# Forward and gradients of attention plus a gated layer, one core: which rows of the query, gate and up weights lie in which partition

## The chip, the cores and the metric

The kernel runs on one core of one Trainium2 chip. The metric is device time in microseconds for one execution; where several runs are given, the median. The engines are TensorE (PE, with its weight loads PEld), VectorE (DVE), ScalarE (ACT), GpSimd (POOL) and SyncE (SP), which here does little but issue transfers. The core's 16 DMA engines move all data between HBM and SBUF (128 partitions).

## The reference, cut to what matters

One token for each of two sequences (B = 2, D = 576) goes through a layer norm; the result feeds a cached attention with 32 query and 16 key/value heads over 4096 positions, and a gated layer with F = 4608. The kernel returns the output and the gradients of eight inputs.

```python
xn  = _layernorm(x)                                   # (2, 1, 576)
q   = xn @ wq                                         # wq (576, 4096)
o   = softmax(q k^T / sqrt(128)) v                    # k, v caches (2, 16, 4096, 128)
att = o @ wo                                          # wo (4096, 576)
h   = (xn @ w_gate) * (xn @ w_up)                     # (576, 4608) each
out = x + att + h @ w_down                            # w_down (4608, 576)
# and jax.vjp of out: gradients of x, k, v, wq, wo, w_gate, w_up, w_down; all bfloat16
```

The caches are read once and gradients of the same size are written once, so the traffic is 92.48 MB read and 92.48 MB written.

## The kernel before, in words

The program is written as a set of Python generators ("streams") that yield their costs to a planner (`Order`). The planner runs while the kernel is built and decides the order in which every engine's instructions are emitted; on the chip that order is fixed. The costs that the streams yield are the same numbers before and after the change.

Nearly all transfers go through SP's queue in the planned order: K and V tiles of 1 MiB (`load_kv`, issued at L1117), weights (`load_w`, L1132 to L1164), and results (`put`, L691). A transfer that SP issues waits behind those issued earlier. Sixteen buffers of 1 MiB (tag `big`) hold K/V tiles, transposed tiles, results on their way out, and the gate and up weights.

A matmul that contracts over D = 576 needs D on the partitions: four chunks of 128 and a rest of 64. Before, chunk c, partition p holds row 128c + p, and the rest of 64 rows is a transfer of its own (the tail):

- query weights, one group of 512 columns out of eight: two tails of 64 rows x 256 columns into partitions 0 to 63 and 64 to 127 (L1132), then the main transfer of 512 rows x 512 columns (L1136), pieces of 1024 bytes;
- gate and up weights, 1024 columns at a time (four times, then once 512): gate main (L1155), gate tail into partitions 0 to 63 of `gu` (L1158), up main (L1155), up tail into partitions 64 to 127 of `gu` (L1158), pieces of 2048 bytes; two transfers of the down weights follow (L1164, pieces of 4608 bytes).

The normalised row has to be laid out in the same way. In `front`, DVE computes `xnb` (2 x 576, L611), PE transposes it chunk by chunk into PSUM (L619 to L621), and DVE copies that to `xs` (L623 to L625), which all products with these weights use. `xnb` is also spread over the partitions (`widen`, L574) to `xnr`, for the outer products of the weight gradients. Later in `front`, x itself is transposed with small matmuls (L645, L648) for the gradient of the layer norm. At the end, `final_dx` brings the summed gradient of xn back into row order with matmuls (L1507, L1510), adds the direct path (`rows_add`, L1455), and `rows_put` copies PSUM to SBUF (L1447 on ACT, L1449 on DVE) and stores the row (L1451).

Of the kernel before, what the change touches and what calls it, by code (L numbers as in the profile page):

```python
# [250 lines left out]
def DVE(cost):  # L251
    return ("op", "DVE", cost)
# [18 lines left out]
def REL(tag, i):  # L271
    return ("rel", tag, i)
# [81 lines left out]
def kernel(  # L354
# [225 lines left out]
    def front_y():  # L580
# [9 lines left out]
                dyT[32 * a:32 * a + 32, :, 0:2].rearrange("p (k e) b -> p k e b", e=2))  # L590
        yield SET(Edy)

    def front():
        xb, yb = xy[:, 0:D], xy[:, D:2 * D]
        for t, src in ((xb, A_x), (yb, grad_out)):
            yield DMA("ACT", 0.45, 2304, 1152)
            nc.scalar.dma_start(t, src.rearrange("b s d -> (b s) d"))
        yield ("lset", Ein)
        yield SPAWN(front_y(), -999.0)
        yield ACT(1.5)  # L600
        nc.scalar.activation(warm[:], eps_t[0:1], AF.Sqrt)
        yield WAIT(Ein)
        yield DVE(1.0)
        for k in range(2):
            nc.vector.bn_stats(bst[:, k], xb[:, k * HD2:(k + 1) * HD2])
        nc.vector.bn_aggr(mv[:], bst[:].rearrange("p k s -> p (k s)"))
        yield ACT(0.3)
        nc.scalar.activation(rstd[:], mv[:, 1:2], AF.Sqrt, bias=eps_t[:], scale=1.0)
        yield DVE(0.6)
        nc.vector.reciprocal(rstd[:], rstd[:])  # L610
        nc.vector.tensor_scalar(xnb[:], xb, mv[:, 0:1], rstd[:], op0=ALU.subtract, op1=ALU.mult)  # L611
        yield ACT(1.5)
        nc.scalar.activation(warm[:], eps_t[0:1], AF.Exp)

        i = yield ACQ("m")
        tp = m_t[i][:].bitcast(BF16)
        yield PE(0.02, 0.16)
        for c in range(4):
            nc.tensor.transpose(tp[:, 2 * c:2 * c + 2], xnb[:, c * P:(c + 1) * P], ident[0:2, 0:2])  # L619
        nc.tensor.transpose(tp[0:64, 8:10], xnb[:, 512:576], ident[0:2, 0:2])  # L620
        nc.tensor.transpose(tp[:, 10:12], xnb[:, 448:576], ident[0:2, 0:2])  # L621
        yield DVE(0.4)
        nc.vector.tensor_copy(xs[:, 0:4, 0:2], tp[:, 0:8].rearrange("p (c b) -> p c b", b=2))  # L623
        nc.vector.tensor_copy(xs[0:64, 4, 0:2], tp[0:64, 8:10])
        nc.vector.tensor_copy(xs[64:128, 5, 0:2], tp[64:128, 10:12])  # L625
        yield REL("m", i)
        yield SET(Exn)
        yield WAIT(Edy)
        yield from widen(xnb, xnr)
        yield SET(Exr)  # L630

        yield PRIO(PR["const"])
        yield WAIT(Econst)
        nr = gg[0:2, 0, 0:4]
        yield DVE(0.3)
        nc.vector.memset(gg[:, 1], 0.0)
        nc.vector.tensor_scalar(nmu[:], mv[:, 0:1], -1.0, None, op0=ALU.mult)
        nc.vector.tensor_scalar(nr[:, 0:2], identf[0:2, 0:2], nmu[:], None, op0=ALU.mult)
        nc.vector.tensor_scalar(nr[:, 2:4], identf[0:2, 0:2], rstd[:], None, op0=ALU.mult)
        i = yield ACQ("m")  # L640
        tp, bp = m_t[i], m_t[i][:, 64:68]
        yield PE(0.0, 0.3)
        for a in range(4):
            for c in range(4):
                nc.tensor.matmul(tp[32 * c:32 * c + 32, 2 * a:2 * a + 2], lhsT=xb[:, P * c + 32 * a:P * c + 32 * a + 32],  # L645
                                 rhs=ident[0:2, 0:2], start=True, stop=True)
        for a in range(2):
            nc.tensor.matmul(tp[0:32, 8 + 2 * a:10 + 2 * a], lhsT=xb[:, 512 + 32 * a:544 + 32 * a],  # L648
                             rhs=ident[0:2, 0:2], start=True, stop=True)
        nc.tensor.matmul(bp, lhsT=view(ones[:], 0, 2, 0, [[0, P]]), rhs=nr, start=True, stop=True)  # L650
        yield DVE(0.9)
        nc.vector.tensor_copy(xnT[:, 0:8], tp[:, 0:8])
        nc.vector.tensor_copy(xnT[0:32, 8:12], tp[0:32, 8:12])
        nc.vector.tensor_copy(nrT[:], bp)
        for k, op in ((0, ALU.add), (2, ALU.mult)):
            nc.vector.tensor_tensor(xnT[:], xnT[:], view(nrT[:], 0, P, k, [[0, 6], [1, 2]]), op)
        nc.vector.memset(gg[:, 0], 0.0)
        yield REL("m", i)
        yield SET(Eprep)
# [448 lines left out]
    def load_kv():  # L1108
        n = 0
        for s in range(NS):  # L1110
            g, b = divmod(s, Bq)
            for t in range(2):
                for l in range(G):
# [6 lines left out]
                    yield SET(issued[n])  # L1120
                    n += 1

    def load_w(item):
        kind, i = item
        if kind in ("wq", "wo"):
            st = grp[i]
            n0 = i * GH * Dh
            st[kind] = w = yield ACQ("ww")
            if kind == "wq":
                for h in range(2):  # L1130
                    yield DMA("SP", 0.36, 64 * 256 * 2, 512)
                    nc.sync.dma_start(ww_t[w][64 * h:64 * h + 64, 4 * FS:WB],  # L1132
                                      A_wq[512:576, n0 + 256 * h:n0 + 256 * h + 256])
                yield ("lset", st["Lq"])
                yield DMA("SP", 0.4, 128 * 4 * FS * 2, 1024)
                nc.sync.dma_start(ww_t[w][:, 0:4 * FS].rearrange("p (c n) -> p c n", n=FS),  # L1136
                                    A_wq[0:512, n0:n0 + FS].rearrange("(c p) n -> p c n", p=P))
                yield ("lset", st["Lm"])
            else:
                yield DMA("SP", 0.36, 128 * GH * D * 2, 4608)  # L1140
                nc.sync.dma_start(ww_t[w][:, 0:GH * D].rearrange("p (c n) -> p c n", c=GH),
                                  A_wo[n0:n0 + FS, :].rearrange("(p c) n -> p c n", c=GH))
                yield ("lset", st["Lo"])
        else:
            halves = range(2 * i, min(2 * i + 2, NFS))
            f0, width = 2 * i * FS, FS * len(halves)
            sl = dict(width=width, n=len(halves), G=[], turned=events(len(halves)))
            sl["gu"] = yield ACQ("gu")
            gu = gu_t[sl["gu"]]
            Lgu = Event()  # L1150
            for w, Wsrc in enumerate((B_w_gate, B_w_up)):
                b = yield ACQ("G")
                sl["G"].append(b)
                yield DMA("SP", 0.4, 128 * 4 * width * 2, 2 * width)
                nc.sync.dma_start(G_t[b][:, 0:4 * width].rearrange("p (c n) -> p c n", n=width),  # L1155
                                  Wsrc[0:512, f0:f0 + width].rearrange("(c p) n -> p c n", p=P))
                yield DMA("SP", 0.36, 64 * width * 2, 2 * width)
                nc.sync.dma_start(gu[64 * w:64 * w + 64, 0:width], Wsrc[512:576, f0:f0 + width])  # L1158
            yield ("lset", Lgu)
            for hh, k in enumerate(halves):  # L1160
                d = yield ACQ("ww")
                Ld = Event()
                yield DMA("SP", 0.36, 128 * FC * D * 2, 4608)
                nc.sync.dma_start(ww_t[d][:, 0:FC * D].rearrange("p (c n) -> p c n", c=FC),  # L1164
                                  B_w_down[k * FS:(k + 1) * FS, :].rearrange("(p c) n -> p c n", c=FC))
                yield ("lset", Ld)
                yield SPAWN(mlp(k, hh, sl, Lgu, Ld, d), pr("mlp", MLP_AT[k] / 4))
# [274 lines left out]
            yield PRIO(pr("front", 2 * g))  # L1442
            yield from group_front(g)

    def rows_put(o, n, out):
        yield ACT(0.4)
        nc.scalar.copy(view(xy[:], 0, 2, n * D, [[P, 5], [1, 64]]), o[0:2, 0, 0:320].rearrange("p (k n) -> p k n", k=5))  # L1447
        yield DVE(0.4)
        nc.vector.tensor_copy(view(xy[:], 0, 2, n * D + 64, [[P, 4], [1, 64]]), o[0:2, 1, 0:256].rearrange("p (k n) -> p k n", k=4))  # L1449
        yield DMA("SP", 0.3, 2304, 1152)  # L1450
        nc.sync.dma_start(out.rearrange("b s d -> (b s) d"), xy[:, n * D:(n + 1) * D])  # L1451

# [5 lines left out]
    def final_out():  # L1458
# [6 lines left out]
        for dc in range(5):  # L1465
# [5 lines left out]
            if dc == 4:  # L1471
                nc.tensor.matmul(o[0:2, 0, 256:320], lhsT=acc[64:P, 4, :], rhs=identf[64:P, 64:P],
                                 start=False, stop=True)
        yield from rows_put(o, 0, out_0)
        yield REL("o", i)

    def final_dx():
# [9 lines left out]
        for k in range(2):  # L1487
            nc.tensor.matmul(mt[0:32, 8:12], lhsT=accx[:, P:160], rhs=F8[:, 4 * k:4 * k + 4],
                             start=(k == 0), stop=(k == 1))
        rows_add(o, 1)  # L1490
        yield DVE(0.5)
        nc.vector.tensor_copy(g[:, 0:8], mt[:, 0:8])
        nc.vector.tensor_copy(g[0:32, 8:12], mt[0:32, 8:12])
# [10 lines left out]
        yield REL("m", m)  # L1504
        yield PE(0.4, 0.3)
        for a in range(4):
            nc.tensor.matmul(view(o[:], 0, 2, 512 * (a // 2) + 32 * (a % 2), [[64, 4], [1, 32]]),  # L1507
                             lhsT=gx[:, 2 * a:2 * a + 2], rhs=identf[:], start=False, stop=(a == 3))
        for a in range(2):
            nc.tensor.matmul(o[0:2, 0, 256 + 32 * a:288 + 32 * a], lhsT=gx[0:32, 8 + 2 * a:10 + 2 * a],  # L1510
                             rhs=identf[0:32, 0:32], start=False, stop=(a == 1))
        yield from rows_put(o, 1, out_1)
        yield REL("o", i)

    od.spawn(front(), -1000.0)
# [43 lines left out]
```

## Time and profile before

| | |
|---|---|
| Median of 3 runs | 477.73 us (476.86 to 479.79) |
| The profiled execution | 480.7 us, span 478.9 us, mean granted PE clock 0.704 |
| Busy: PE, DVE, ACT, POOL | 375.8, 369.2, 335.6, 152.0 us |
| SP's queue | 41848 packets, 184.96 MB, packets fill 98.3% of 16 engines' span |
| Main transfers that the change touches | query 8 x 512 KB; gate and up 8 x 1024 KB and 2 x 512 KB |
| Tails that it touches | query 16 x 32 KB; gate and up 8 x 128 KB and 2 x 64 KB |

A packet is one contiguous piece that one DMA engine moves. The page gives for each queue the time that its packets took as a share of the span of 16 engines; 100% means that on average 16 packets are always under way. A window answer gives, for a stretch of the span, the busy time of each engine with its number of instructions, the granted PE clock, the share of the DMA engines' time that packets took, and the GB/s that they moved. Packets are counted where they start, so a share of a short stretch can be a little over 1.

### The profile page before, as it was taken

How to read it: one execution, taken by the hardware profiler on the slowest of the kernel's cores; microseconds unless marked ns; L12 is line 12 of the kernel's file. 1: busy time of each engine (PE TensorE's matmuls, PEld its weight loads, DVE VectorE, ACT ScalarE, POOL GpSimd, SP SyncE). 2: the span in 40 equal slices, each digit the busy share in tenths (PEclk: the TensorE clock that was granted, in tenths of full speed). 3: DMA queues.
4: the chain of work that ended last, by engine and by line, in shares of the span. 5: the costliest groups of instructions: out<-in, count | busy, mean ns of one | idle time of the engine just before them, and what ended most of it. 6: DMA issues, size and time to landing. Idle time of an engine off the chain costs nothing.

```text
span 478.9 us, 15380 instructions
## 1 busy us (share of the span) xinstructions
PE 375.8 (78%) x6538; PEld 214.9 (45%) x6538; DVE 369.2 (77%) x708; ACT 335.6 (70%) x507; POOL 152.0 (32%) x208
## 2 busy tenths in 40 slices
PE   1668588989878877768878986599887769898894
PEld 1545353545554534446344453464444424444452
DVE  8788787867867976786956987889677958888781
ACT  3139659966787693833869875399776978897871
POOL 0440074343003643003434530032644556333000
PEclk9979676556766677885567595859656876656876
DMA  8999999999999999999999999999999999999994
GB/s 299 355 405 419 391 402 380 353 377 422 422 400 371 395 365 393 423 414 389 316 399 384 354 402 422 421 413 406 346 414 415 418 419 422 419 417 391 425 369 187
DMA packets 41925, 185.95 MB, mean 388 GB/s; under 512 B 3960, under 2 KB 13440, under 8 KB 25472
## 3 DMA queue, kind: packets, MB, share of 16 engines
q1 hardware_dynamic: 41848, 184.96, 98.3%
q8 instruction: 51, 0.84, 0.7%
q14 instruction: 18, 0.15, 0.1%
q10 hardware_dynamic: 8, 0.00, 0.0%
HBM read 92.48 MB, written 92.48 MB: 386 GB/s over the span
## 4 chain that ended last, share of the span: by engine, by line
DMA 46%; PE 25%; DVE 14%; ACT 8%; issue 3%; SPq 2%; POOL 1%; DVEq 0%; ACTq 0%; POOLq 0%
DMA out_dram<-big 18%; DMA big<-in_A_v_cache_dram 15%; DVE big L464 8%; ACT big L468 7%; PE ps_o L1255 4%; DMA big<-in_A_k_cache_dram 4%; PE ps_m L1234 4%; PE ps_m L1407 4%; PE ps_o L722 3%; DMA gu<-in_B_w_up_dram 3%; DMA ww<-in_A_wo_dram 3%; DMA big<-in_B_w_gate_dram 2%; DVE big L470 2%; PE ps_m L678 1%; PE ps_o L759 1%
## 5 line engine op out<-in xcount | busy, mean ns | idle before, releaser
L468 ACT CAST big<-ps_o 128x1024 bf16<-128x1024 f32 (+2 forms) x310 | 277.6, 958 | 47.6 <-PE ps_o L1255 18.9
L464 DVE STREAM_TRANSPOSE big<-big 128x1024 f32<-128x1024 f32 x146 | 175.9, 1224 | 29.7 <-DMA out_dram<-big 16.2
L1222 POOL TENSOR_TENSOR BD<-vr,mask 128x2048 bf16<-128x2048 bf16 x32 | 115.3, 3603 | 105.4 <-ACT vr L468 49.8
L470 DVE CAST big<-ps_o 128x1024 bf16<-128x1024 f32 (+2 forms) x68 | 74.2, 1093 | 16.4 <-PE ps_o L722 7.4
L1234 PE MATMUL ps_m<-big,W 128*32 128x128 bf16 x2048 | 59.9, 282 | 11.3 <-DVE cr L1359 2.6
L1234 PEld LDWEIGHTS <-W 128*32 128x32 bf16 x2048 | 46.7, 125 | 27.9 <-issue 25.7
L1255 PE MATMUL ps_o<-BD,dd 32*128 32x512 bf16 x256 | 45.8, 480 | 9.9 <-ACT big L468 7.9
L671 POOL COPY wt<-wm 64x128 bf16<-64x128 bf16 (+1 forms) x34 | 8.9, 261 | 138.2 <-DVE wm L664 119.5
L1255 PE MATMUL ps_o<-BD,pp 32*128 32x512 bf16 x256 | 48.2, 520 | 5.5 <-ACT big L468 4.0
L1199 POOL COPY W<-rep 32x16 bf16<-32x16 bf16 x128 | 24.5, 192 | 55.8 <-DVE rep L983 33.6
L464 DVE STREAM_TRANSPOSE big<-ww 128x1152 f32<-128x1152 f32 x25 | 34.0, 1359 | 7.7 <-DMA ww<-in_B_w_down_dram 3.5
L1407 PE MATMUL ps_m<-big,pp 128*32 128x512 bf16 x256 | 30.2, 547 | 3.8 <-DMA big<-in_A_v_cache_dram 3.3
L1255 PEld LDWEIGHTS <-dd 32*128 32x128 bf16 x256 | 12.2, 98 | 32.1 <-issue 27.6
L1407 PE MATMUL ps_m<-big,dd 128*32 128x512 bf16 x256 | 25.8, 491 | 0.4 <-DVE oT L1427 0.2
L1255 PEld LDWEIGHTS <-pp 32*128 32x128 bf16 x256 | 10.4, 97 | 28.1 <-issue 24.2
L872 PE MATMUL ps_m<-big,Wdy 128*128 128x128 bf16 x162 | 15.4, 269 | 4.8 <-DVE rz L1320 3.1
L722 PE MATMUL ps_o<-dyr,hb 32*32 32x288 bf16 x288 | 18.0, 382 | 0.2 <-ACT big L468 0.2
L759 PEld LDWEIGHTS <-xnr 32*128 32x128 bf16 x368 | 12.9, 116 | 10.8 <-issue 9.7
L722 PE MATMUL ps_o<-dyr,R 32*32 32x288 bf16 x256 | 16.2, 378 | 1.3 <-ACT big L468 0.9
L872 PEld LDWEIGHTS <-Wdy 128*128 128x128 bf16 x162 | 13.6, 121 | 6.8 <-issue 6.7
L759 PE MATMUL ps_o<-D,xnr 32*128 32x128 bf16 x256 | 13.0, 276 | 3.9 <-issue 2.2
L1308 ACT COPY mr<-m 1x128 f32<-1x128 f32 x16 | 4.7, 295 | 15.8 <-DVE m L1306 15.6
(205 smaller groups left out, 487.3 us busy)
## 6 DMA issues: line engine op xcount, KB each, us to landing
out_dram<-big SPq DMA_DIRECT2D x74, 1024.0 KB, 12.8
big<-in_A_k_cache_dram SPq DMA_DIRECT2D x32, 1024.0 KB, 12.7
big<-in_A_v_cache_dram SPq DMA_DIRECT2D x32, 1024.0 KB, 13.2
out_dram<-big SPq DMA_DIRECT2D x17, 576.0 KB, 10.7
ww<-in_B_w_down_dram SPq DMA_DIRECT2D x9, 576.0 KB, 13.5
ww<-in_A_wo_dram SPq DMA_DIRECT2D x8, 576.0 KB, 7.3
ww<-in_A_wq_dram SPq DMA_DIRECT2D x8, 512.0 KB, 8.0
big<-in_B_w_gate_dram SPq DMA_DIRECT2D x4, 1024.0 KB, 12.3
```

The costliest lines, as they stand in the source:

```text
L464: nc.vector.transpose(out, in_)
L468: nc.scalar.copy(out, in_)
L470: nc.vector.tensor_copy(out=out, in_=in_)
L671: nc.gpsimd.tensor_copy(view(Wt[:], 64 * h, 64, 0, [[dims[-1][1], n], [1, dims[-1][1]]]), view(Wm[:], 64 * h, 64, off, dims))
L722: nc.tensor.matmul(o[32 * q:32 * q + 32, aa, 0:HD2], lhsT=view(t, 32 * q, 32, 2 * A + aa, [[4, 32]]), rhs=dyr[32 * q:32 * q + 32, k * HD2: ...
L759: nc.tensor.matmul(o[:, aa, j * P:(j + 1) * P], lhsT=xnr[32 * a:32 * a + 32, dc * P:(dc + 1) * P], rhs=rhs(a), start=True, stop=True)
L872: nc.tensor.matmul(dh, lhsT=Wdy[:, e, 2 * k:2 * k + P], rhs=view(X[:], 0, P, 64 * k + e, [[D, FC], [2, 32]]), start=(k == 0 and e == 0), s ...
L1199: nc.gpsimd.tensor_copy(view(W_t[t][w][:], 32 * a, 32, 6 + 8 * a, [[G * WW, 4], [WW, G], [1, 2]]), view(rep_t[grp[g]["qs"]][:], 32 * a, 32 ...
L1222: nc.gpsimd.tensor_tensor(BD_t[i][:], view(vr_t[v][:], 0, P, 0, [[0, 16], [1, Dh]]), view(mask16[:], 0, P, 0, [[1, 16], [0, Dh]]), ALU.mult)
L1234: nc.tensor.matmul(sc[32 * cq:32 * cq + 32, :], lhsT=view(W[:], 0, P, (be * G + l) * WW + 6 - 4 * c2 - 2 * l, [[1, 32]]), rhs=view(X[:], 0 ...
L1255: nc.tensor.matmul(o[:, k, :], lhsT=pr2[32 * c4:32 * c4 + 32, :], rhs=BD[32 * c4:32 * c4 + 32, 8 * l + 4 * h2:8 * l + 4 * h2 + 4, :], star ...
L1407: nc.tensor.matmul(ct[32 * j:32 * j + 32, :], lhsT=view(rT, 0, P, 4 * c + 2 * l, [[1, 32]]), rhs=kv_t[kvS[s][t][l]][:, Dh * c:Dh * (c + 4) ...
```

## The change

The rows of the three weights are dealt out anew. Both the main and the tail view of a weight now begin with a dimension of 16: block e has rows 36e to 36e + 35. Of each block, the first 32 rows go to the main transfer and fill partitions 8e to 8e + 7 with four neighbouring rows each; the last 4 go to the tail and fill four partitions of its 64. So partition 8e + j, chunk c holds row 36e + 4j + c. Sizes, pieces, number and order of the transfers stay; the destinations are the same buffers.

Everything that has to agree with this is laid out to match: a permuted copy `xp` of the normalised row (in the third `BD` buffer, before it is first needed) is what PE transposes, a permuted copy of x takes the place of `xb` in the later transposes, and `final_dx` writes its sums through strided views into row order, so that the copies out become contiguous. `xnb` is still computed, after `xs`.

```diff
+    def by_rows(dst, src):
+        return [(view(dst, 0, 2, 0, [[P, 4], [8, 16], [1, 8]]), view(src, 0, 2, 0, [[1, 4], [36, 16], [4, 8]])),
+                (view(dst, 0, 2, 512, [[4, 16], [1, 4]]), view(src, 0, 2, 32, [[36, 16], [1, 4]]))]
...
     def front():
         xb, yb = xy[:, 0:D], xy[:, D:2 * D]
+        xp = BD_t[-1][0:2].rearrange("p a n -> p (a n)")[:, 0:D]
...
-        nc.vector.tensor_scalar(xnb[:], xb, mv[:, 0:1], rstd[:], op0=ALU.subtract, op1=ALU.mult)
+        for d, r in by_rows(xp, xb):
+            nc.vector.tensor_scalar(d, r, mv[:, 0:1], rstd[:], op0=ALU.subtract, op1=ALU.mult)
...
-            nc.tensor.transpose(tp[:, 2 * c:2 * c + 2], xnb[:, c * P:(c + 1) * P], ident[0:2, 0:2])
+            nc.tensor.transpose(tp[:, 2 * c:2 * c + 2], xp[:, c * P:(c + 1) * P], ident[0:2, 0:2])
...
         nc.vector.tensor_copy(xs[64:128, 5, 0:2], tp[64:128, 10:12])
+        nc.vector.tensor_scalar(xnb[:], xb, mv[:, 0:1], rstd[:], op0=ALU.subtract, op1=ALU.mult)
...
         yield DVE(0.3)
+        for d, r in by_rows(xp, xb):
+            nc.vector.tensor_copy(d, r)
...
+    def main_rows(A):
+        return A.rearrange("(e r) n -> e r n", e=16)[:, 0:32, :].rearrange("e (j c) n -> e j c n", c=4)
+
+    def tail_rows(A):
+        return A.rearrange("(e r) n -> e r n", e=16)[:, 32:36, :]
...
-                                      A_wq[512:576, n0 + 256 * h:n0 + 256 * h + 256])
+                                      tail_rows(A_wq[:, n0 + 256 * h:n0 + 256 * h + 256]))
...
-                                    A_wq[0:512, n0:n0 + FS].rearrange("(c p) n -> p c n", p=P))
+                                    main_rows(A_wq[:, n0:n0 + FS]))
...
-                                  Wsrc[0:512, f0:f0 + width].rearrange("(c p) n -> p c n", p=P))
+                                  main_rows(Wsrc[:, f0:f0 + width]))
...
-                nc.sync.dma_start(gu[64 * w:64 * w + 64, 0:width], Wsrc[512:576, f0:f0 + width])
+                nc.sync.dma_start(gu[64 * w:64 * w + 64, 0:width], tail_rows(Wsrc[:, f0:f0 + width]))
...
     def final_dx():
-        rows_add(o, 1)
+        for k in range(2):
+            nc.tensor.matmul(o[0:2, k, 0:HD2], lhsT=ident[0:2, 0:2], rhs=xy[:, D + HD2 * k:D + HD2 * (k + 1)],
+                             start=True, stop=False)
...
-            nc.tensor.matmul(view(o[:], 0, 2, 512 * (a // 2) + 32 * (a % 2), [[64, 4], [1, 32]]),
-                             lhsT=gx[:, 2 * a:2 * a + 2], rhs=identf[:], start=False, stop=(a == 3))
+            nc.tensor.matmul(view(o[:], 0, 2, 512 * (a // 2) + 144 * (a % 2), [[1, 4], [36, 4], [4, 8]]),
+                             lhsT=gx[:, 2 * a:2 * a + 2], rhs=identf[:], start=False, stop=False)
```

In the emitted program the engines' instructions stand in the same order as before. DVE has four more (672 become 676): one `tensor_scalar` of 2 x 576 becomes two of 2 x 512 and 2 x 64, `xnb` follows later as a third, and two copies of x are added. PE, ACT, POOL and SP have as many as before.

More of the change, by code (lines that the diff above doesn't have):

```diff
@@ L618, in front @@
         for c in range(4):
-            nc.tensor.transpose(tp[:, 2 * c:2 * c + 2], xnb[:, c * P:(c + 1) * P], ident[0:2, 0:2])
-        nc.tensor.transpose(tp[0:64, 8:10], xnb[:, 512:576], ident[0:2, 0:2])
-        nc.tensor.transpose(tp[:, 10:12], xnb[:, 448:576], ident[0:2, 0:2])
+            nc.tensor.transpose(tp[:, 2 * c:2 * c + 2], xp[:, c * P:(c + 1) * P], ident[0:2, 0:2])
+        nc.tensor.transpose(tp[0:64, 8:10], xp[:, 512:576], ident[0:2, 0:2])
+        nc.tensor.transpose(tp[:, 10:12], xp[:, 448:576], ident[0:2, 0:2])
         yield DVE(0.4)
@@ L644, in front @@
             for c in range(4):
-                nc.tensor.matmul(tp[32 * c:32 * c + 32, 2 * a:2 * a + 2], lhsT=xb[:, P * c + 32 * a:P * c + 32 * a + 32],
+                nc.tensor.matmul(tp[32 * c:32 * c + 32, 2 * a:2 * a + 2], lhsT=xp[:, P * c + 32 * a:P * c + 32 * a + 32],
                                  rhs=ident[0:2, 0:2], start=True, stop=True)
         for a in range(2):
-            nc.tensor.matmul(tp[0:32, 8 + 2 * a:10 + 2 * a], lhsT=xb[:, 512 + 32 * a:544 + 32 * a],
+            nc.tensor.matmul(tp[0:32, 8 + 2 * a:10 + 2 * a], lhsT=xp[:, 512 + 32 * a:544 + 32 * a],
                              rhs=ident[0:2, 0:2], start=True, stop=True)
@@ L1443, in fronts, with rows_put @@
             yield from group_front(g)
-    def rows_put(o, n, out):
+    def rows_put(o, n, out, parts):
         yield ACT(0.4)
-        nc.scalar.copy(view(xy[:], 0, 2, n * D, [[P, 5], [1, 64]]), o[0:2, 0, 0:320].rearrange("p (k n) -> p k n", k=5))
+        nc.scalar.copy(*parts[0])
         yield DVE(0.4)
-        nc.vector.tensor_copy(view(xy[:], 0, 2, n * D + 64, [[P, 4], [1, 64]]), o[0:2, 1, 0:256].rearrange("p (k n) -> p k n", k=4))
+        nc.vector.tensor_copy(*parts[1])
         yield DMA("SP", 0.3, 2304, 1152)
@@ L1473, in final_out @@
                                  start=False, stop=True)
-        yield from rows_put(o, 0, out_0)
+        yield from rows_put(o, 0, out_0, [
+            (view(xy[:], 0, 2, 64 * k, [[P, 5 - k], [1, 64]]),
+             o[0:2, k, 0:320 - 64 * k].rearrange("p (k n) -> p k n", k=5 - k)) for k in range(2)])
         yield REL("o", i)
@@ L1506, in final_dx @@
         for a in range(4):
-            nc.tensor.matmul(view(o[:], 0, 2, 512 * (a // 2) + 32 * (a % 2), [[64, 4], [1, 32]]),
-                             lhsT=gx[:, 2 * a:2 * a + 2], rhs=identf[:], start=False, stop=(a == 3))
+            nc.tensor.matmul(view(o[:], 0, 2, 512 * (a // 2) + 144 * (a % 2), [[1, 4], [36, 4], [4, 8]]),
+                             lhsT=gx[:, 2 * a:2 * a + 2], rhs=identf[:], start=False, stop=False)
         for a in range(2):
-            nc.tensor.matmul(o[0:2, 0, 256 + 32 * a:288 + 32 * a], lhsT=gx[0:32, 8 + 2 * a:10 + 2 * a],
-                             rhs=identf[0:32, 0:32], start=False, stop=(a == 1))
-        yield from rows_put(o, 1, out_1)
+            nc.tensor.matmul(view(o[:], 0, 2, 512 * a + 32, [[36, 8], [1, 4]]), lhsT=gx[0:32, 8 + 2 * a:10 + 2 * a],
+                             rhs=identf[0:32, 0:32], start=False, stop=True)
+        yield from rows_put(o, 1, out_1, [(xy[:, D + HD2 * k:D + HD2 * (k + 1)], o[0:2, k, 0:HD2]) for k in range(2)])
         yield REL("o", i)
```

## The prediction

> **What bounds the kernel now.** First the page's table of slices, the queue table and the shares of the chain that ended last:
>
> ```profile
> DMA  8999999999999999999999999999999999999994
> GB/s 299 355 405 419 391 402 380 353 377 422 422 400 371 395 365 393 423 414 389 316 399 384 354 402 422 421 413 406 346 414 415 418 419 422 419 417 391 425 369 187
> q1 hardware_dynamic: 41848, 184.96, 98.3%
> DMA 46%; PE 25%; DVE 14%; ACT 8%; issue 3%; SPq 2%; POOL 1%; DVEq 0%; ACTq 0%; POOLq 0%
> ```
>
> The DMA engines are busy in every slice, and packets of SP's queue fill 98.3% of their time. PE (78% of the span) and DVE (77%) are not far behind, but DMA ends the largest part of the chain. Yet the rate moves between 316 and 425 GB/s while the engines stay busy: some packets take longer than others of their size. So I count DMA time as span, microsecond for microsecond: what the packets take longer, summed over all and divided by 16, the span grows; only the 1.7% without packets (8 us) could take some of it.
>
> Then the windows over the loads of gate and up weights: for each of the four full loads one row in the gate main transfer, one just behind it, one at the up tail (columns: stretch; length and busy time of PE, PEld, DVE, ACT, POOL; PE clock, DMA share, GB/s):
>
> ```profile
> 11.10:13.40 2.30, 0.71 (x12) 0.48 (x10) 1.59 (x3) 0.68 (x2) 0.00 (x0) 1.00 1.02 401
> 13.60:14.90 1.30, 0.00 (x0) 0.00 (x0) 1.30 (x2) 0.00 (x0) 0.00 (x0) 1.00 1.08 265
> 17.60:18.90 1.30, 1.30 (x35) 1.10 (x28) 1.30 (x1) 0.00 (x0) 1.30 (x1) 1.00 1.06 282
> 91.10:93.40 2.30, 1.43 (x41) 1.10 (x41) 1.85 (x3) 1.92 (x3) 1.42 (x1) 0.50 1.02 403
> 93.90:95.40 1.50, 1.50 (x36) 0.88 (x34) 1.14 (x2) 1.50 (x2) 0.00 (x0) 0.50 1.08 221
> 98.10:99.40 1.30, 1.30 (x10) 0.23 (x9) 1.13 (x1) 1.30 (x4) 1.03 (x6) 0.50 1.06 258
> 170.10:172.40 2.30, 1.89 (x27) 1.05 (x31) 2.26 (x4) 2.30 (x5) 1.10 (x5) 0.71 1.02 401
> 172.80:174.10 1.30, 1.30 (x42) 0.91 (x34) 0.94 (x1) 1.15 (x2) 1.30 (x1) 0.50 1.12 258
> 178.90:180.20 1.30, 0.00 (x0) 0.00 (x0) 0.28 (x1) 1.30 (x3) 0.00 (x0) 1.00 1.10 248
> 270.10:272.40 2.30, 2.30 (x30) 1.09 (x33) 2.02 (x4) 2.16 (x5) 0.39 (x2) 0.50 1.01 392
> 272.70:273.90 1.20, 1.20 (x45) 0.89 (x41) 1.14 (x2) 0.87 (x2) 0.18 (x1) 0.50 1.11 261
> 276.30:277.50 1.20, 1.12 (x18) 0.81 (x15) 1.12 (x3) 1.04 (x2) 1.16 (x3) 0.76 1.17 304
> ```
>
> The gate main transfer, 128 partitions, runs at 392 to 403 GB/s. At each tail, 64 partitions, the rate falls to 221 to 304 (mean of the eight 262) with the DMA share still at 1.06 or more: the engines are not idle, they wait inside their packets. By the trace's packet records a packet of 2048 bytes takes 84 ns in the gate mains (median, all four) and 173, 145, 108 and 148 ns (means) in the gate tails; up mains and the first down transfer, which start while other engines are still in a tail, are slowed with them.
>
> Two readings fit. The destination: 64 partitions, so several engines write into the same part of SBUF and share its entry. Or the source: rows 512 to 575, close together in HBM. The change keeps the first (same 64 partitions) and takes away the second. I hold the first: the down and output weights also read 576 KB in one piece, and away from tails their packets of 4608 bytes take 178 ns, the shortest there is. That reading makes the main transfers matter.
>
> **Part one: main transfers.** Before, source and destination both begin with 128; now the source begins with 16 blocks. If each engine takes one block, engine e writes the neighbouring partitions 8e to 8e + 7. No row tells which engine writes which partitions today; the rows tell that the dealing for 128 partitions costs the mains nothing (392 to 403 GB/s) and that the loads of the same pieces into 64 partitions cost a third of the rate. So I price the new mains by the nearest rows, the dips, between no conflict (0) and the deepest dip over the whole transfer (221 GB/s).
>
> [...]
>
> I choose the value so: engines are about as far apart in time in a main as in a tail (a gate main's packets span 2.8 to 3.5 us, for 2.7 us of work each), and engines out of step pay less. So I take the mean dip, 262 GB/s.
>
> - Gate and up: 8 x 1024 + 2 x 512 KB = 9.44 MB. At 399 GB/s (mean of the four mains) 23.7 us, at 262 it is 36.0: +12.4 us. At 221: +19.0.
> - Query: 8 x 512 KB = 4.19 MB. A packet of 1024 bytes takes 46 ns (median), so 16 engines move 356 GB/s: 11.8 us. At 262: 16.0, +4.2 us. At 221: +7.2.
>
> Sum +16.6 us, bounds 0 and +26.2. Late next are the K, V and store transfers behind each of these 18 mains on SP's queue, then what needs them.
>
> **Part two: tails.** Same destinations, other rows. If the dips come from the destination: 0. If from the rows, they go: what packets took beyond the shortest usual duration of their size sums in the five loads to 1.9, 2.2, 2.4, 1.4 and 0.3 us (divided by 16), 8.2 in all. I take 0 and keep -8.2. Neighbouring rows in the query mains could save at most what all 1024-byte packets lose: (49.7 - 46) ns x 8448 / 16 = 2.0 us.
>
> **Part three: the front.** From the timeline of DVE and PE (start, duration in us):
>
> ```profile
> 8.15 0.42 DVE L611 TENSOR_SCALAR xnb<-xy,mv,rstd 2x576 bf16<-2x576 bf16 x1
> 10.42 0.12 DVE L623 COPY xs<-ps_m 128x8 bf16<-128x8 bf16 x1
> 10.60 0.68 PE L966 MATMUL ps_m<-xs,ww 128*128 128x2 bf16 x20 [0.96 <-DVE xs L624]
> ```
>
> Ahead of `xs`, the 0.42 us of `xnb` become two permuted writes: 0.42 x 512/576 = 0.37, and 0.12 for the small one (as the small copy L623), so +0.1; scattered elements are in no row, at twice the time +0.5. `xnb` comes 2.7 us later (behind the copies from 10.42 on, and ahead of a 1.25 us transpose), and with it PE's spread (L574) and `xnr`. Queued behind L574 on PE is the first query product L966: it waits for `xnb` and for L574 (0.6 us), some 1.0 us, with ACT's qr and POOL's first W copies (15.46) behind it. Two copies of x add 0.5 us to DVE at 15.3. Together up to 2.0 us on the first scores, once. The cover is SP's queue: by 11.2 us it holds transfers that land 16 us later. I take +0.3 us, bounds 0 and 2.0. The third `BD` buffer, where `xp` lies, is not due before POOL's third build, which starts after 45 us.
>
> **Part four, at nothing:** `final_dx` has as many matmuls (two of 288 columns for 320 and 256), and the two row copies (0.41 us each) become contiguous; after the row's store at 473.8 the last stores run to 478.9, which covers 0.3 us either way. Issuing: a changed main takes SP 0.4 to 1.1 us now; doubled, 18 of them cost at most 20 us of SP, whose issues land 12 us and more later (median of the mains of gate and up).
>
> **Sum.** 480.7 (profiled execution; span 478.9 and 1.8 around it) + 16.6 + 0.3 = 497.6 us. The median of the runs, 477.73, lies 3.0 below that execution, so 494.6.
>
> **Rivals.** A. The forecast: mains at the tails' rate, slower. For it: the dips at a full DMA share; against it: no main has ever been dealt so. Own range 484 to 506 (from a third of the sum to both upper bounds). Chance 0.74.
>
> B. No conflict: the blocks are only other addresses, or neighbours drift apart and never meet. For it: the query tails, 64 partitions too, show no slow packets (27 ns, median and nearly all); they are 512 bytes long, though, and over in 0.1 us. 477.7 + 0.3 = 478.0, between 475 and 482. Chance 0.15. That the queue ignores the block form and deals as today is the same case.
>
> C. The other side: faster, because the dips come from rows 512 to 575. Place: the eight full tails. With the tail's rows spread over the whole matrix no dip is left: 477.7 - 8.2 + 0.3 = 469.8, with the query's 2.0 us 467.8. It decides as soon as packets in a gate tail are back at 84 ns. Against it: the 4608-byte rows above, and that the dips last into transfers of other rows. [...] Chance 0.11.
>
> **How the numbers follow.** Faster by over 1%, which is about what a measurement of this kernel can tell from no change: most of C, 0.10. Within 1%: nearly all of B, a little of C and of A's low end, 0.15. Slower: 0.75. The range runs from B's middle to A's upper end, 478 to 506; C, half of B and conflicts beyond the mean are the 2 in 10 outside.
>
> **What would show it.** A: gate and up mains at 220 to 300 GB/s with a full DMA share, 2048-byte packets at 130 to 150 ns, 1024-byte ones over 60, mean rate down from 388 to some 375 GB/s. B: the four main rows still near 400 and the dips still there. C: the dips gone. Wrong altogether: DMA shares well under 1 in the mains (SP or the queue too slow), or the first scores late by more than 2 us.

## The result, and the profile after

The change makes the kernel slower: 513.34 us (median of 4 runs, 511.64 to 515.91) against 477.30 before in the same comparison, a ratio of 1.075, 95% interval 1.0687 to 1.0812. That is +36.0 us where +16.9 was predicted (494.6), and beyond the upper end of the range, 506.

The slices, SP's queue and the shares of the chain that ended last, of the kernel after:

```profile
DMA  8999999999999999999899899999999999999995
GB/s 280 241 385 378 360 412 419 306 274 424 420 410 335 411 252 227 426 420 371 329 325 399 323 225 411 424 416 411 383 294 414 424 417 413 425 423 356 417 384 199
q1 hardware_dynamic: 41848, 184.96, 99.1%
DMA 56%; PE 20%; DVE 12%; ACT 6%; issue 3%; SPq 2%; POOL 1%; DVEq 0%; ACTq 0%; POOLq 0%
```

The packets and the bytes are the same as before to the last digit, and packets fill still more of the engines' time. Away from the weights the rate is what it was (410 to 426 GB/s). What is new are deep slices: 241, 274, 252, 227, 225, where before no slice but the first and the last was below 316. DMA ends 56% of the chain, 46% before.

The windows over the same loads show what lies in these slices. For the first, second and fourth full load there are three rows each: in the gate main, around the gate tail, in the up main; for the third one in the gate main (columns as in the prediction: stretch; length and busy time of PE, PEld, DVE, ACT, POOL; PE clock, DMA share, GB/s):

```profile
12.00:15.50 3.50, 1.38 (x26) 0.90 (x25) 2.23 (x4) 1.32 (x3) 0.00 (x0) 1.00 1.06 214
16.50:17.80 1.30, 0.62 (x20) 0.54 (x20) 1.26 (x8) 0.00 (x0) 0.95 (x5) 1.00 1.08 217
18.00:21.50 3.50, 3.46 (x83) 3.08 (x82) 3.43 (x6) 0.00 (x1) 3.47 (x2) 1.00 1.06 211
97.00:101.00 4.00, 3.94 (x67) 1.54 (x59) 3.64 (x7) 3.24 (x4) 0.00 (x0) 0.50 1.04 210
102.70:104.00 1.30, 1.30 (x10) 0.14 (x8) 0.96 (x1) 1.30 (x4) 1.05 (x7) 0.50 1.05 217
104.50:108.50 4.00, 2.39 (x29) 1.10 (x27) 2.56 (x3) 2.36 (x5) 1.84 (x1) 0.50 1.08 214
182.00:187.00 5.00, 4.46 (x77) 2.31 (x76) 1.99 (x4) 4.07 (x8) 3.85 (x4) 0.50 1.07 180
294.30:298.30 4.00, 4.00 (x81) 2.20 (x78) 3.66 (x9) 2.97 (x5) 0.83 (x2) 0.50 1.06 212
298.80:300.00 1.20, 1.20 (x13) 0.22 (x9) 1.20 (x3) 0.27 (x1) 1.20 (x1) 0.50 1.07 212
300.00:304.00 4.00, 3.49 (x45) 2.37 (x45) 3.81 (x6) 3.73 (x8) 1.86 (x5) 0.91 1.07 219
```

The mains, 392 to 403 GB/s before, run at 180 to 219 with a DMA share of 1.04 and more: the engines are as busy as before and move half as much. Main and tail can no longer be told apart by the rate. Where a load stood out as a short dip, it is now one stretch of 10 us and more at about half the rate.

By the trace's packet records, with the durations of each size summed and divided by 16 engines:

| bytes in a packet | what it carries | before, us | after, us | difference | mean of one, ns |
|---|---|---|---|---|---|
| 512 | query tails | 1.8 | 2.1 | +0.3 | |
| 1024 | query mains, last gate and up load, smaller results | 26.3 | 33.2 | +6.9 | 49.7 → 62.9 |
| 2048 | gate and up, main and tail | 28.8 | 47.3 | +18.5 | 100 → 164 |
| 4608 | down and output weights, their gradients | 53.6 | 59.8 | +6.2 | 197 → 220 |
| 8192 | K, V and large results | 328.4 | 331.2 | +2.8 | |
| all, other sizes included | | 470.8 | 506.1 | +35.3 | |

The span grew by 31.8 us (478.9 to 510.7). The rest of the 35.3 came out of time without packets: 1.7% of the span before, 8.1 us, and 0.9% after, 4.6 us. That the two add up is arithmetic, as a span is packet time plus time without packets. What they say is that the time without packets did not grow: the loss lies inside packets, and no wait for a compute engine is needed to explain it. (The medians differ by 4 us more than the spans because the execution profiled before was 3.4 us slower than its median.) 25.4 us lie in packets of 1024 and 2048 bytes, the sizes of the changed mains (3200 of the 8448 packets of 1024 bytes are results on their way out; those that start more than 6 us from a query tail went from 48 to 50 ns only). 9.0 us lie in packets of 4608 and 8192 bytes, whose transfers were not changed at all. The packet records also tell where: packets of 4608 bytes that start within 1 us of one of 2048 bytes went from 224 to 270 ns in the mean, those of 8192 bytes from 337 to 405; further than that from the gate and up loads, and more than 6 us from any query tail, they stayed at 184 and 186, and at 320 and 318.

### The profile page after: what moved, and what is told of

It is laid out like the page before. It is cut to its first block, busy times and chain, and to the rows that moved or that the text cites. A ratio compares the mean times of both kernels' runs of the same rounds, so it can differ in the third digit from the quotient of the medians.

```text
span 510.7 us, 15384 instructions
## 1 busy us (share of the span) xinstructions
PE 382.9 (75%) x6538; PEld 217.6 (43%) x6538; DVE 370.1 (72%) x712; ACT 336.4 (66%) x507; POOL 152.0 (30%) x208
## 4 chain that ended last, share of the span: by engine, by line
DMA 56%; PE 20%; DVE 12%; ACT 6%; issue 3%; SPq 2%; POOL 1%; DVEq 0%; ACTq 0%; POOLq 0%
DMA out_dram<-big 18%; DMA big<-in_A_v_cache_dram 10%; DMA big<-in_A_k_cache_dram 10%; DMA big<-in_B_w_up_dram 9%; DVE big L464 8%; DMA ww<-in_A_wo_dram 6%; ACT big L468 5%; PE ps_o L1270 3%; DMA big<-in_B_w_gate_dram 3%; PE ps_o L731 3%; PE ps_m L1422 3%; PE ps_m L1249 3%; DVE big L470 1%; PE ps_m L687 1%; PE ps_o L768 1%
## 5 line engine op out<-in xcount | busy, mean ns | idle before, releaser
L1249 PE MATMUL ps_m<-big,W 128*32 128x128 bf16 x2048 | 58.8, 278 | 15.3 <-DVE cr L1374 6.7
L1249 PEld LDWEIGHTS <-W 128*32 128x32 bf16 x2048 | 45.5, 122 | 31.4 <-issue 29.4
L1270 PE MATMUL ps_o<-BD,dd 32*128 32x512 bf16 x256 | 49.3, 518 | 9.3 <-ACT big L468 7.6
L1422 PE MATMUL ps_m<-big,pp 128*32 128x512 bf16 x256 | 28.9, 528 | 6.1 <-DVE pp L464 3.2
L866 ACT COPY gs<-ps_m 128x256 f32<-128x256 f32 x9 | 3.4, 376 | 27.4 <-PE ps_m L863 27.4
L881 PE MATMUL ps_m<-big,Wdy 128*128 128x128 bf16 x162 | 17.9, 297 | 3.3 <-DVE rz L1335 1.6
L881 PEld LDWEIGHTS <-Wdy 128*128 128x128 bf16 x162 | 15.9, 136 | 5.8 <-issue 5.8
```

The lines of the kernel that those rows point to most:

```text
L881: nc.tensor.matmul(dh, lhsT=Wdy[:, e, 2 * k:2 * k + P], rhs=view(X[:], 0, P, 64 * k + e, [[D, FC], [2, 32]]), start=(k == 0 and e == 0), s ...
L1249: nc.tensor.matmul(sc[32 * cq:32 * cq + 32, :], lhsT=view(W[:], 0, P, (be * G + l) * WW + 6 - 4 * c2 - 2 * l, [[1, 32]]), rhs=view(X[:], 0 ...
L1270: nc.tensor.matmul(o[:, k, :], lhsT=pr2[32 * c4:32 * c4 + 32, :], rhs=BD[32 * c4:32 * c4 + 32, 8 * l + 4 * h2:8 * l + 4 * h2 + 4, :], star ...
L1422: nc.tensor.matmul(ct[32 * j:32 * j + 32, :], lhsT=view(rT, 0, P, 4 * c + 2 * l, [[1, 32]]), rhs=kv_t[kvS[s][t][l]][:, Dh * c:Dh * (c + 4) ...
```

## The experiments

Two theories. **Destination**: with 16 blocks in front, the transfer would be dealt to the engines block by block, engine e would get partitions 8e to 8e + 7, and engines would collide at the destination (D in the expectations). **Source**: the new order of rows in HBM (36 neighbouring rows for each engine) would read badly (S). Ratios are to runs of the kernel before on the same chip (medians 477.85 to 478.22), with 95% intervals.

### 1. Same kind of rows, 32 blocks

```diff
-        return A.rearrange("(e r) n -> e r n", e=16)[:, 0:32, :].rearrange("e (j c) n -> e j c n", c=4)
+        return A.rearrange("(e r) n -> e r n", e=32)[:, 0:16, :].rearrange("e (j c) n -> e j c n", c=4)
...
-        return A.rearrange("(e r) n -> e r n", e=16)[:, 32:36, :]
+        return A.rearrange("(e r) n -> e r n", e=32)[:, 16:18, :]
```

(from the kernel after; `by_rows` and the views in `final_dx` follow, so the whole layer is computed)

> The same idea with 32 blocks of 18 rows (16 for the main transfer, 2 for the tail) instead of 16 blocks of 36: rows of a partition are neighbours in HBM as in the changed kernel, the normalised row is laid out to match, but the leading dimension of the source is 32, so a block fills four partitions. Theory D (destination: which engine writes which partitions): 16 leading blocks force eight neighbouring partitions on one engine; with 32 the queue can deal as it does for 128, so mains at about 400 GB/s, 2048-byte packets back at 84 ns (median), and the time of the kernel before, 478 us (475 to 482). Theory S (source: neighbouring rows of one engine collide in HBM): still neighbouring rows, so 505 to 515 us and packets near 165 ns.

Measured: 478.80 us, ratio 1.0005 (0.9977 to 1.0033). The gate mains of loads 1, 2 and 4, each in the first row, with the tail behind the second and the fourth (windows of this kernel):

```profile
11.00:13.30 2.30, 1.45 (x26) 0.89 (x25) 1.85 (x4) 0.85 (x2) 0.00 (x0) 1.00 1.04 399
91.00:93.30 2.30, 1.41 (x38) 0.90 (x37) 2.12 (x3) 1.76 (x3) 1.54 (x1) 0.63 1.02 400
93.90:95.40 1.50, 1.50 (x36) 0.86 (x35) 1.14 (x4) 1.50 (x3) 0.00 (x0) 0.50 1.07 251
267.30:269.60 2.30, 2.30 (x35) 1.08 (x39) 2.02 (x5) 2.16 (x4) 0.23 (x2) 0.50 1.03 402
269.80:271.00 1.20, 1.20 (x43) 0.94 (x37) 1.14 (x2) 0.79 (x2) 0.26 (x1) 0.50 1.09 224
```

Blocks of 18 neighbouring rows, and the mains are back at 399 to 402 GB/s with the tails' dips as before. The whole loss is gone through the number of blocks, 32 in place of 16. Every other part of the change (scattered writes, the late `xnb`, strided matmul outputs) is still in this kernel.

### 2, 3 and 4. One half of the change at a time

In 2 the query weights, in 3 the gate and up weights, in 4 all three are loaded as before; the rest is as after. For the query weights:

```diff
-                                    main_rows(A_wq[:, n0:n0 + FS]))
+                                    A_wq[0:512, n0:n0 + FS].rearrange("(c p) n -> p c n", p=P))
```

(tails likewise)

> The changed kernel with the query weights loaded as before (their rows then do not match the layout of the normalised row). By the packet records gate and up packets (2048 bytes) cost 18.5 us more in the changed kernel, and of the 6.2 us that 4608-byte packets cost more the larger part are down weights behind them: theory D 502 to 506 us. If the 36 us were mostly something else (front, issue, query), under 495.

> The changed kernel with gate and up weights loaded as before (their rows then do not match). 1024-byte packets cost 6.9 us more in the changed kernel, 512-byte ones 0.3, output weights behind them perhaps 2: theory D 485 to 488 us. If query and gate/up add up, this and the gate-and-up-only run together lose what the changed kernel loses, 36 us.

> The changed kernel with all weights loaded as before: only the permuted rows in the front and the strided writes at the end are left (products then use rows that do not match). Forecast's parts three and four: 477.6 us, within 2 us of the kernel before. If the front costs real time: 480 or more.

Measured: gate and up alone 499.09 us, ratio 1.041 (1.0377 to 1.0443), +20.9 us. Query alone 489.42, ratio 1.0213 (1.018 to 1.0246), +11.2. Layout alone 478.09, ratio 0.9992 (0.9968 to 1.0016).

The layout costs nothing that can be measured. The query half costs nearly three times what the prediction gave the query mains (4.2): the packets of 1024 bytes alone account for 6.6 (32.9 us for 26.3), those of 4608 bytes for another 3.1 (56.7 for 53.6): the output weights, loaded next to the query weights, land 9.7 us after their issue and not 7.3. Both misses against the expectations, one down and one up, are a few us. Together the two halves make 32.1 of the 36.0. The other 4 are little more than the noise (the interval of the ratio after against before allows 32.8 to 38.8 us), but the packets of 4608 bytes show a gap too (+1.6 in experiment 2, +3.1 in 3, +6.2 in both). Why is open.

### 5. Sixteen blocks without neighbouring rows

```diff
-                                  Wsrc[0:512, f0:f0 + width].rearrange("(c p) n -> p c n", p=P))
+                                  Wsrc[0:512, f0:f0 + width].rearrange("(r e) n -> e r n", e=16).rearrange("e (j c) n -> e j c n", c=4))
```

(from the kernel before, query main alike; block e takes rows e, e + 16, e + 32 ...)

> The kernel before with its tails untouched, and the mains dealt with 16 leading rows: block e has rows e, e + 16, e + 32 and so on, so every engine's rows are spread over the whole 512 and the rows under way at one time lie side by side (the layout of the normalised row isn't changed with it, so products use rows that don't match). Theory D: the leading 16 decides, whatever the rows: 2048-byte packets near 165 ns, 1024-byte ones over 60 on average, 508 to 516 us as the changed kernel. Theory S (an engine's neighbouring rows are the trouble): no engine has neighbouring rows, so 476 to 482 us.

Measured: 514.35 us, ratio 1.0775 (1.0738 to 1.0813). The four gate mains:

```profile
12.40:16.40 4.00, 0.47 (x5) 0.29 (x5) 0.21 (x1) 0.59 (x2) 0.00 (x0) 1.00 1.04 201
100.00:104.00 4.00, 3.85 (x47) 1.53 (x42) 3.64 (x7) 3.56 (x5) 0.00 (x0) 0.50 1.05 167
185.00:189.00 4.00, 3.82 (x69) 2.40 (x73) 2.42 (x5) 4.00 (x7) 2.72 (x5) 0.50 1.07 209
296.00:300.00 4.00, 4.00 (x81) 2.20 (x78) 3.71 (x7) 2.99 (x5) 0.89 (x2) 0.50 1.07 214
```

No two rows of a block are neighbours here, and the loss is as large as in the kernel after, at much the same rates and DMA shares. With experiment 1 this settles the source theory: neighbouring rows are neither needed for the loss (5) nor enough for it (1). What both bad kernels share is a source view that begins with 16. That engines then meet at the destination is the reading of theory D; these runs show the form that costs, not the place where packets wait.

### 6. Tails over 128 partitions

```diff
-                nc.sync.dma_start(gu[64 * w:64 * w + 64, 0:width], Wsrc[512:576, f0:f0 + width])
+                nc.sync.dma_start(gu[:, w * width // 2:(w + 1) * width // 2], Wsrc[448:576, f0:f0 + width // 2])
```

(from the kernel before: as many bytes, in pieces of 1024)

> The kernel before with the gate and up tails written to all 128 partitions: the same bytes per tail, as 128 pieces of 1024 bytes (rows 448 to 575, half the columns) instead of 64 of 2048; the products of the tails then use other rows. Theory D: the dips behind the tails are the 64 partitions', so they go: of the 8.2 us that packets lose in these loads some 1 is left, and the smaller pieces cost (2 x 46 - 84) ns x 576 / 16 = 0.3 us more: 469 to 473 us. Theory S (rows 512 to 575 are the trouble): the same rows are still read by all engines at once, dips and 478 us stay.

Measured: 472.51 us, ratio 0.9901 (0.988 to 0.9921). The last 64 rows are still read (half of their columns), and the dips are gone: 2048-byte packets, now of mains only, take 86 ns in the mean, and those of 4608 bytes 189 where they took 197. Around the first two gate tails (265 and 221 GB/s in the kernel before):

```profile
13.80:15.10 1.30, 0.00 (x0) 0.00 (x0) 1.30 (x5) 0.00 (x0) 0.00 (x0) 1.00 1.07 386
91.70:93.00 1.30, 1.30 (x36) 0.88 (x34) 0.94 (x2) 1.30 (x2) 0.00 (x0) 0.50 1.06 391
```

As these tails read only half as many bytes of the last 64 rows, this run alone would not clear the rows. Experiment 1 does: its tails take rows from all over the matrix into 64 partitions, and the dips stay (251 and 224 GB/s). The dips of the kernel before are the 64 partitions', not the rows'.

### 7. Only the tails dealt anew

```diff
-                nc.sync.dma_start(gu[64 * w:64 * w + 64, 0:width], Wsrc[512:576, f0:f0 + width])
+                nc.sync.dma_start(gu[64 * w:64 * w + 64, 0:width], Wsrc[:, f0:f0 + width].rearrange("(e r) n -> e r n", e=16)[:, 32:36, :])
```

(from the kernel before, query tails alike)

> The kernel before with only the tails of query, gate and up dealt as in the changed kernel (last 4 of each 36 rows; the normalised row isn't laid out to match, so these products use rows that don't match). Theory D: the destination is the same 64 partitions, so the dips stay: 475 to 480 us, gate tail packets still at 140 ns and more. Theory S: the rows of a tail now lie all over the matrix, so the dips go: 468 to 472 us.

Measured: 474.26 us, ratio 0.9938 (0.9913 to 0.9962), a gain that the destination theory as I held it did not give. Just behind the gate main of loads 1 and 2:

```profile
13.30:14.60 1.30, 0.00 (x0) 0.00 (x0) 1.30 (x5) 0.06 (x1) 0.00 (x0) 1.00 1.08 298
91.20:92.70 1.50, 1.50 (x40) 0.86 (x34) 1.18 (x2) 1.38 (x2) 0.00 (x0) 0.50 1.06 329
```

The dips are shallower (265 and 221 GB/s in these places before), and packets of the four gate tails take 114, 101, 121 and 123 ns in the mean (173, 145, 108 and 148 before; the same form as before takes 98 to 201 in the traces of experiments 3 and 4, so single tails scatter). So the form that halves the mains' rate is the milder one for the tails. It could still be the rows, which this edit spreads too.

### 8. The two tails one behind the other

In `load_w`, the gate tail is issued behind the up main, next to the up tail (from the kernel before):

```diff
-                nc.sync.dma_start(gu[64 * w:64 * w + 64, 0:width], Wsrc[512:576, f0:f0 + width])
+                if w == 1:
+                    for v, W in enumerate((B_w_gate, B_w_up)):
+                        nc.sync.dma_start(gu[64 * v:64 * v + 64, 0:width], W[512:576, f0:f0 + width])
```

> The kernel before with the gate tail moved behind the up main on SP's queue, right ahead of the up tail; every other instruction stays in its place. Theory D: engines that are not in step then write one tail into the lower 64 partitions and the other into the upper 64 at the same time, and the up main no longer runs into a tail: the loss of 8.2 us falls by a third to a half: 473 to 476 us. Theory S: the rows are the same and read closer together: 478 us or more.

Measured: 477.09 us, ratio 0.9978 (0.9955 to 1.0001). A miss: no gain that can be told from none. The packets of up tails take 129 to 157 ns here (103 to 124 before), so about half of what the gate tails no longer lose (84 to 88 ns here) is lost there.

### 9 and 10. Tails in 16 blocks, inside the last 64 rows

```diff
+    def tail_rows(A):
+        return A[512:576].rearrange("(j e) n -> e j n", e=16)
...
-                nc.sync.dma_start(gu[64 * w:64 * w + 64, 0:width], Wsrc[512:576, f0:f0 + width])
+                nc.sync.dma_start(gu[64 * w:64 * w + 64, 0:width], tail_rows(Wsrc[:, f0:f0 + width]))
```

(from the kernel before, query tails alike; mains untouched; three small copies on DVE and a strided view in `final_dx` match it, so the whole layer is computed. Experiment 10 adds the edit of 8.)

> A version meant to be used: the kernel before with only its tails dealt with 16 leading rows (row 512 + 16 j + e in partition 4 e + j), the 64 tail values of the normalised row copied into that order by three small DVE copies, and the sums written back through strided views. From the run with only the tails dealt anew (0.994 of the kernel before): 0.992 to 0.997 of the kernel before, about 475 us, gate tail packets at 100 to 125 ns instead of 108 to 173. If that gain was the rows' (spread over the whole matrix there, inside the last 64 rows here): no gain, 478 us.

> As the version before it, with the gate tail moved behind the up main, next to the up tail. If the two tails then write into different halves at the same time, another 1 to 2 us less, 473 to 474 us; the run with tails together and the old dealing gained 0.2% at most, so no change against the version before it is nearly as likely.

Measured: 474.88 us, ratio 0.9938 (0.9914 to 0.9962), and 474.58 us, ratio 0.9919 (0.9891 to 0.9948). Experiment 9 reads the same 64 rows as the kernel before and gains what 7 gained, with gate tails at 117, 114, 114 and 120 ns: the gain is the dealing's. Both beat the kernel before by some 3 us; they can't be told from each other.

### 11. The loads by themselves

Only loads of 1 MiB (512 rows x 1024 columns of gate and up weights) in four forms, and of 64 rows in others, with nothing beside them; zeros are stored at the end. It was run once.

> No layer is computed (the results are zeros): only loads of gate and up weights, one stage of 8 MiB or 4 MiB after the other on SP's queue, then stores of zeros. Theory D: 128 leading rows 380 to 400 GB/s (packets 84 ns), 16 blocks of 36 rows 200 to 230 GB/s (packets near 150 ns and more), 32 blocks of 18 rows as 128, 16 leading rows spread over the matrix as 16 blocks; 64-row loads into the lower 64 partitions 200 to 230 GB/s in either dealing, and into lower and upper 64 in turn between 230 and 390. Theory S: the stages with 16 blocks of neighbouring rows and the 64-row loads slow, 32 blocks slow too, spread rows fast.

Measured, one window each (length, busy DVE and POOL, clock, DMA share, GB/s): 128 rows in front, 16 blocks of 36 rows, 32 blocks of 18, 16 blocks of interleaved rows, two stretches with 64-row loads into the lower partitions dealt in the two ways, and one with such loads into the lower and upper 64 in turn:

```profile
5.30:21.50 16.20, 0.00 (x0) 0.00 (x0) 1.00 1.05 389
28.80:57.70 28.90, 0.00 (x0) 0.00 (x0) 1.00 1.06 217
87.40:103.60 16.20, 0.00 (x0) 0.00 (x0) 1.00 1.05 386
110.90:139.80 28.90, 0.00 (x0) 0.00 (x0) 1.00 1.07 218
167.70:176.50 8.80, 0.00 (x0) 0.00 (x0) 1.00 0.64 177
179.40:188.30 8.90, 0.00 (x0) 0.00 (x0) 1.00 0.61 178
212.70:221.40 8.70, 0.00 (x0) 0.00 (x0) 1.00 0.62 179
```

The four main forms give two rates: 389 and 386 GB/s (a 2048-byte packet 88 ns), 217 and 218 (164 ns). Here form decides, rows don't, and neither compute nor other traffic is needed for it. Nor is a lower PE clock (0.674 granted in the kernel after, 0.704 before): here it is 1.00 throughout. The 64-row stretches missed the expectation (177 to 179 GB/s for 200 to 230, and for 230 to 390 in turn) and say nothing about dealing: at a DMA share of 0.61 to 0.64 the engines waited for work. SP issued the 16 loads of the second stretch 0.74 us apart, and 128 KB in 0.74 us are 177 GB/s.

## Why the prediction was right or wrong

**What bounds the kernel: right.** Packet time counted as span, and what the idle 1.7% could take it took, 3.5 us of it.

**The reading of the dips: right in its main part.** Rival C is refuted by experiment 1, where the tails' rows are spread and neither the dips nor the time change; the gain that spread rows seemed to bring in 7 comes without spreading in 9. B is refuted by the mains at 180 to 219 GB/s.

**Part one, price of the mains: here the prediction failed.** The loss came where it was expected, in the mains at a full DMA share, and its size was wrong. The step is "engines out of step pay less. So I take the mean dip, 262 GB/s". Its first half was an estimate that no row showed, and the mean dip mixes the tail's packets with those of the main behind it: a window of 1.3 us holds both, and so does its rate. Loads dealt so run at 217 GB/s by themselves (experiment 11), for which the deepest dip, 221, was the nearest row. At 217, 9.44 MB take 43.5 us and 4.19 MB 19.3: +19.8 and +7.5, together +27.3 in place of 16.6; measured are +25.4 in the packets of these sizes, less in part because the up mains were not at their best before either (99 to 116 ns a packet; with the tails over 128 partitions, experiment 6, all mains took 86 in the mean). The query mains of the kernel after that stand alone in time take 70 to 83 ns a packet of 1024 bytes (47 to 58 before), and 217 GB/s are 75.5. That engines drift apart and pay less did not come about: over 28.9 us of such loads alone the mean packet stays at 160 ns, its median at 164.

Which engine writes which partition is in no record of these traces. That engines collide at an entry to SBUF fits the rates, 217 and 218 GB/s with 16 in front, 386 and 389 with 32 and 128 (experiment 11); it is a reading, argued and not seen.

**A term that was missing: the neighbours.** The sum priced only the changed transfers. Transfers of K, V, down and output weights that are under way at the same time take longer too: +6.2 us in packets of 4608 bytes and +2.8 in those of 8192, 9.0 in all. 27.3 + 9.0 = 36.3, and the medians differ by 36.0; so close a fit is partly luck, as the packets of all four sizes add up to 34.4 and the profiled spans differ by 31.8. The prediction had the row for it (transfers behind a tail "are slowed with them") and used it only as evidence.

**Part two, tails: 0, nearly right.** Dealt anew in 16 blocks they gain 3 to 4 us when the mains are left alone (7 and 9), through the dealing, which the prediction had ruled out by "Same destinations"; the bound of -8.2 covered it. In the kernel after, gate tails take 148 to 176 ns, among gate mains of 152 to 176, and nothing of this gain is to be seen.

**Parts three and four: right.** The first query product starts at 12.15 us in the trace after and 10.60 before, 1.5 us later, more than the 1.0 expected of it, and yet the layout by itself costs nothing that can be measured (experiment 4, where this product starts at 12.15 too). That SP's queue is what covered it, as the prediction has it, was not tested. From the timeline of the kernel after:

```profile
11.12 0.42 DVE L632 TENSOR_SCALAR xnb<-xy,mv,rstd 2x576 bf16<-2x576 bf16 x1
11.59 0.63 PE L574 MATMUL ps_o<-xnb,sel 2*128 2x288 bf16 x2 [2.32 <-DVE xnb L632]
12.15 0.70 PE L975 MATMUL ps_m<-xs,ww 128*128 128x2 bf16 x20
```

**What would show it.** The full DMA share and 1024-byte packets over 60 ns (62.9) came true; 130 to 150 ns for 2048 bytes became 164, 220 to 300 GB/s became 180 to 219, and the mean rate fell to 364, not 375. The range's upper end was the sum at the deepest dip and the front's bound, without neighbours; with them it would have held the result.

## What to carry to other kernels

Where a load is rearranged, look at which dimension both sides of the transfer begin with before looking at the rows: here loads alone ran at 386 to 389 GB/s with 128 or 32 in front of the source view and at 217 to 218 with 16, for the same bytes, partitions and piece size. The sign to look for is a low GB/s at a full DMA share; price such a form at its deepest row, not at a mean over windows that mix it with other packets, and add what the transfers beside it lose. A short tail into half of the partitions is worth a look of its own: spread over all of them, or dealt in 16 blocks, it gave back 0.6 to 1.0% here.

## What of the hardware was not expected

- Loads of 1 MiB into 128 partitions alone on the chip ran at two rates: 386 to 389 GB/s with 128 and 32 in front of the source view, 217 to 218 with 16, whichever rows they took.
- The same 16 in front that nearly halves the rate of a 128-partition load (217 for 389 GB/s) is the milder form for 64 partitions: gate tails 114 to 120 ns a packet against 108 to 173, and 474.88 us for the kernel against 478.0 before. Why is open.
- Beside the slowed transfers others took longer too: packets of 4608 bytes, in transfers that were not touched, went from 197 to 220 ns in the mean, from 224 to 270 next to the gate and up loads, and stayed at 184 to 186 away from the changed loads.
- Loads of 128 KB one behind another, alone, kept the engines only 0.61 to 0.64 busy (177 to 179 GB/s); in the second such stretch SP issued them 0.74 us apart.
